# Three more PSUM banks for the MoE groups of a fused attention and two-MoE kernel, from the attention's end on

## The chip, the cores and the metric

The kernel runs on one core of one Trainium2 chip, in one launch. The metric is the device time in microseconds (us). The kernel before takes 1096.97 us, the median of three runs (1094.63 to 1098.74).

## What is computed

An attention with rotary position embedding (4 batches, 8 heads, 576 positions, 64 dimensions per head), and behind it two MoE blocks on its 2304 tokens of 512 numbers each. All in float32:

```python
def _attn_ref(q, k, v):
    ...
    q_rot, k_rot = (rotate(q), rotate(k))
    scores = scale * np.matmul(q_rot, k_rot.transpose(0, 1, 3, 2))
    scores = scores - np.max(scores, axis=-1, keepdims=True)
    attn = np.exp(scores)
    attn = attn / (np.sum(attn, axis=-1, keepdims=True) + 1e-09)
    return np.matmul(attn, v).astype(np.float32)

def _moe_ref(x, w1, w2, w3, w_out):        # d_ff = 768
    h = np.maximum(np.maximum(x @ w1, x @ w2), x @ w3)
    return (h @ w_out).astype(np.float32)

def _moe2_ref(x, w_in, w_out):             # d_ff = 2048
    h = x @ w_in
    g = h * (1.0 / (1.0 + np.exp(-h)))
    return (g @ w_out).astype(np.float32)
```

## The kernel before

**Numbers in two halves.** Every float32 operand of a MoE is kept as a high and a low float16 half of the scaled number, and a product is three float16 matmuls (high by high, high by low, low by high) that add up in PSUM. GpSimd or ScalarE makes the high half (`split`, L154 and L156), VectorE the low one (L159).

**Groups.** `group` (L502 to L506) takes a tile of one PSUM bank (128 x 512 float32) and adds a list of matmuls up in it. All matmuls of both MoEs but those of the last product are made by it, so they all have line 505. Its bank comes from the ring `ps_m`, which has two. The same ring serves `all_max` (L112), which finds the largest number over all partitions for a scale.

**PSUM has eight banks.** During the attention two are `ps_m`'s, three hold the scores (`ps_s`, one tile), two the transposes (`ps_t`), one the product with v (`ps_x`). The last three pools are closed with the attention (L879). `ps_o` (L899, three banks, for the last product) takes three of those six afterwards.

**The attention** goes tile by tile through scores (L354 to L364), maximum (L374, VectorE), exponential (L381, ScalarE), norm (L393), transposes (L422) with their copies (L426, L428), and the product with v (`av`, L437 to L447).

**The first MoE** (`moe1`) works on one batch at a time, in two halves of 256 and 320 tokens. `up(half, f)` makes three groups of 12 matmuls for each of six pieces f of d_ff, one for each of w1, w2, w3. The first result is read out of PSUM by ScalarE (`t`, L521), the other two by VectorE (`t`, L523), which takes the maximum with the t before. Then the halves of h are made: the high one by ScalarE (L529), the low one by VectorE (L530). `down(half)` makes four groups of 18 matmuls from h, read by ScalarE (`y`, L547) and stored in DRAM. Batch 3 runs in this order: up(0, f) for six f, up(1, 0), down(0), up(1, f) for the other five f, down(1). While it runs, the weights of the second MoE are loaded (L688) and split (L690), one piece for each group (L889 to L897), and its first block of 512 tokens is loaded (L703) and split (`y_split`).

**The second MoE** (`moe2`) takes five blocks of tokens (four of 512, one of 256). `s1` makes 16 groups for a block; ScalarE reads each with the Silu (`gt`, L735), VectorE makes both halves of g from it (L158, L159). `s2` makes the last product for 128 tokens at a time, 48 matmuls of 512 columns in a bank of `ps_o` (L749); VectorE reads it (`ob`, L751), and a DMA stores it (L762).

**What sets the order.** The source gives the data flow and a program order. The tile framework lays the instructions into each engine's queue when the kernel is built: of what is ready by its own model of time, the earlier in the program goes first. So the queue of an engine can differ from the program order, and it can change when buffers are added. A pool's memory is given to a later pool once the tiles in it have had their last reader.

Of the kernel before, what the change touches and what calls it, by code (L numbers as in the profile page):

```python
# [7 lines left out]
F32 = mybir.dt.float32  # L8
# [6 lines left out]
PSUM = bass.MemoryType.PSUM  # L15
DRAM = bass.MemoryType.DRAM

P = 128
# [4 lines left out]
def fused_kernel(  # L23
# [51 lines left out]
    ps_m = Ring(ctx, "ps_m", 2, space=PSUM)  # L75
# [423 lines left out]
    w1_scale = {}  # L499
    WO1 = Weights(wp1, "wo1", NF1, DM)  # L500

    def group(passes, n):  # L502
        ps = ps_m.tile([P, 512], F32, tag="m", name="m")
        for i, (l, r) in enumerate(passes):
            nc.tensor.matmul(ps[:, 0:n], l, r, start=(i == 0), stop=(i == len(passes) - 1))  # L505
        return ps  # L506

    def moe1(b, pools):
# [5 lines left out]
        def up(half, f):  # L514
            o, n = PARTS[half][:2]
            part = []

            def evac(e, ps):
                t = tmp_p.tile([P, n], F32, tag="t", name="t")
                if e == 0:  # L520
                    nc.scalar.activation(out=t, in_=ps[:, 0:n], func=AF.Copy, scale=2.0 ** -22)  # L521
                else:
                    nc.vector.scalar_tensor_tensor(  # L523
                        out=t, in0=ps[:, 0:n], scalar=2.0 ** -22, in1=part[-1], op0=ALU.mult, op1=ALU.max
                    )
                part.append(t)
                if e == 2:
                    hh = h1[half, f] = h1_p.tile([P, 2, n], F16, tag="h1", name="h1")
                    nc.scalar.activation(out=hh[:, 0], in_=t, func=AF.Copy)  # L529
                    nc.vector.tensor_tensor(out=hh[:, 1], in0=t, in1=hh[:, 0], op=ALU.subtract)  # L530

            for e in range(3):
                passes = []
                for c in range(KC):
                    i, fo = (f // FG * KC2 + c // 2) * 3 + e, (c % 2 * FG + f % FG) * P
                    wh, wl = W1.h(i)[:, fo:fo + P], W1.l(i)[:, fo:fo + P]
                    passes += [(wh, x[:, c, 0, o:o + n]), (wh, x[:, c, 1, o:o + n]), (wl, x[:, c, 0, o:o + n])]
                yield half, n * len(passes), False
                ps = group(passes, n)
                evac(e, ps)  # L540

        def down(half):
            o, n = PARTS[half][:2]

            def evac(m, ps):
                ysb = pools[2].tile([P, n], F32, tag="y", name="y")
                nc.scalar.activation(out=ysb, in_=ps[:, 0:n], func=AF.Copy, scale=cy_t[b])  # L547
                nc.sync.dma_start(out=yscr[:, m, b * S + o:b * S + o + n], in_=ysb)

            for m in range(KC):  # L550
                passes = []
                for f in range(NF1):
                    wh = WO1.h(f)[:, m * P:(m + 1) * P]
                    wl = WO1.l(f)[:, m * P:(m + 1) * P]
                    h = h1[half, f]
                    passes += [(wh, h[:, 0]), (wh, h[:, 1]), (wl, h[:, 0])]
                yield half, n * len(passes), True
                ps = group(passes, n)
                evac(m, ps)
# [160 lines left out]
    def moe2(st, pools, ps_o, wi_rest, wo_all):  # L720
# [3 lines left out]
        def s1(j, f):  # L724
            yt, sg, ch = yts[j]
            n = blocks[j][1]
            wi = st["wi"]
            passes = []
            for c in range(KC):
                i, fo = (f // 4) * KC + c, (f % 4) * P  # L730
                wh, wl = wi.h(i)[:, fo:fo + P], wi.l(i)[:, fo:fo + P]
                passes += [(wh, yt[:, 0, c]), (wh, yt[:, 1, c]), (wl, yt[:, 0, c])]
            ps = group(passes, n)
            gt = gt_p.tile([P, n], F32, tag="gt", name="gt")
            nc.scalar.activation(out=gt, in_=ps[:, 0:n], func=AF.Silu, scale=ch)  # L735
            g = gs[j, f] = g_p.tile([P, 2, n], F16, tag="g", name="g")
            split(g[:, 0], g[:, 1], gt, sg, "dve")
# [139 lines left out]
    for _ in wprep3:  # L877
        pass
    attn_pools.close()  # L879
    while nxt[0] < B - 1:  # L880
        nxt = next(moe)
    w2_p = Ring(ctx, "w2_p", 1, side="right")
# [62 lines left out]
```

## Time and profile before

| | |
|---|---|
| median of three runs | 1096.97 us (1094.63 to 1098.74) |
| the profiled execution | 1101.35 us, its span 1099.6 us |
| mean granted TensorE clock | 0.963 |
| TensorE busy | 1011.0 us (92% of the span) |
| VectorE, ScalarE, GpSimd busy | 570.9, 486.9, 241.9 us |
| last matmul of the attention | near 643 us |
| first matmul of the second MoE | 718.35 us |

The engines are called PE (TensorE matmul), PEld (TensorE's load of weights), DVE (VectorE), ACT (ScalarE), POOL (GpSimd) and SP (the queue that issues DMAs) in the rows. The granted clock is a share of 2.4 GHz, so 0.50 is 1.2 GHz. Matmuls are pipelined, so that a row's duration is a little longer than its distance to the next. The time of a run holds 1 to 2 us around the span.

### The profile page before, as it was taken

To read this page: it belongs to the slowest core of one execution; us is meant where nothing else is said; L and a number is where in the kernel's file an instruction comes from. 1 tells how busy PE (TensorE), PEld (TensorE's weight loads), DVE (VectorE), ACT (ScalarE), POOL (GpSimd) and SP (SyncE) were. 2 spreads that over 40 slices of the span, in tenths; PEclk is the share of its full clock that TensorE was granted. 3 is DMA by queue.
4 is the path that set the end of the run, shared out by engine and by line. 5 is a ranking of instruction groups with operands and counts; after the bars stand their busy time and mean duration, and the time that the engine had idled before them with its cause. 6 is when DMAs were issued, how large, how long until landed. Compare 5 with 4: busy or idle time off the path is not lost.

```text
span 1099.6 us, 16116 instructions
## 1 busy us (share of the span) xinstructions
PE 1011.0 (92%) x6138; PEld 628.7 (57%) x6138; DVE 570.9 (52%) x1124; ACT 486.9 (44%) x1184; POOL 241.9 (22%) x259
## 2 busy tenths in 40 slices
PE   2478898999988999989999888999999999999997
PEld 1244675676775766757767566644444444444554
DVE  5868666434587465466456568424434223423322
ACT  3678675655756567646666731122112012101111
POOL 1595126620146631041111116100000000000000
PEclk9589997999999899989999999999999999999999
DMA  7633032300334423122223263000101000100000
GB/s 193 194 108 125 13 92 50 103 1 7 103 90 133 116 88 100 43 85 87 64 87 105 78 274 129 7 19 5 54 10 49 20 20 1 39 20 1 20 20 20
DMA packets 79389, 76.09 MB, mean 69 GB/s; under 512 B 44752, under 2 KB 61648, under 8 KB 78288
## 3 DMA queue, kind: packets, MB, share of 16 engines
q1 hardware_dynamic: 75760, 65.03, 19.6%
q10 hardware_dynamic: 3552, 10.03, 2.7%
q8 instruction: 48, 0.79, 0.3%
q14 instruction: 29, 0.24, 0.1%
HBM read 57.21 MB, written 17.83 MB: 68 GB/s over the span
## 4 chain that ended last, share of the span: by engine, by line
PE 73%; DVE 4%; POOL 3%; DMA 2%; issue 1%; SPq 1%; ACT 0%; DVEq 0%; POOLq 0%
PE m L505 36%; PE o L749 17%; PE xp L441 6%; PE s L364 5%; PE tr L422 4%; POOL wi L156 1%; PE xp L437 1%; DVE wi L159 1%; PE s L361 1%; PE tr L328 1%; PE s L354 1%; POOL qk L316 1%; DVE nb L374 1%; POOL w L312 0%; SPq L272 0%
## 5 line engine op out<-in xcount | busy, mean ns | idle before, releaser
L505 PE MATMUL m<-x,w 128*128 128x320 f16 (+1 forms) x1632 | 232.6, 290 | 9.9 <-DVE t L523 6.6
L749 PE MATMUL o<-wo,g 128*128 128x512 f16 x828 | 193.2, 379 | 0.0
L505 PEld LDWEIGHTS <-w 128*128 128x128 f16 x1632 | 160.0, 99 | 55.6 <-issue 15.7
L505 PE MATMUL m<-yt,wi 128*128 128x512 f16 (+1 forms) x920 | 189.8, 358 | 0.0
L735 ACT ACTIVATE gt<-m,ch 128x512 f32<-128x512 f32 (+1 forms) x80 | 51.5, 644 | 297.0 <-PE m L505 282.6
L749 PEld LDWEIGHTS <-g 128*128 128x128 f16 x864 | 84.5, 98 | 99.7
L505 PEld LDWEIGHTS <-wi 128*128 128x128 f16 x920 | 89.7, 98 | 89.3
L374 DVE TENSOR_REDUCE nb<-s 128x2 f32<-128x1152 f32 (+1 forms) x80 | 98.8, 1235 | 64.7 <-PE s L364 48.2
L381 ACT ACTIVATE e<-s,nb 128x576 f32<-128x576 f32 x144 | 105.3, 737 | 44.4 <-DVE nb L374 40.0
L158 DVE TENSOR_SCALAR g<-gt,sg 128x512 f16<-128x512 f32 (+1 forms) x80 | 36.7, 458 | 162.9 <-ACT gt L735 162.9
L422 PE MATMUL tr<-ident,e 128*128 128x128 f32 x576 | 100.5, 292 | 17.3 <-ACT pt L426 4.6
L393 ACT ACTIVATE e<-e,rec 128x576 f32<-128x576 f32 x144 | 104.3, 767 | 19.1 <-DVE rec L391 18.9
L207 POOL TENSOR_SCALAR z<-z 128x256 uint16<-128x256 uint16 x64 | 54.9, 857 | 258.6 <-DVE z L206 240.2
L422 PEld LDWEIGHTS tr<-ident,e 128*128 128x128 f32 x576 | 70.5, 148 | 39.6 <-ACT pt L426 9.7
L364 PE MATMUL s<-T 64*128 64x512 f32 (+2 forms) x384 | 85.7, 525 | 0.0
L426 ACT ACTIVATE pt<-tr 128x384 f32<-128x384 f32 x128 | 61.1, 487 | 54.4 <-PE tr L422 53.9
L441 PE MATMUL xp<-pt,vd 128*64 128x256 f32 (+1 forms) x512 | 85.2, 432 | 0.0
L505 PE MATMUL m<-h,wo 128*128 128x256 f16 (+1 forms) x512 | 73.2, 289 | 1.0 <-DVE wo L159 1.0
L364 PEld LDWEIGHTS s<-T 64*128 64x128 f32 x384 | 47.4, 200 | 28.6 <-issue 7.9
L523 DVE SCALAR_TENSOR_TENSOR t<-m,t 128x256 f32<-128x256 f32 (+1 forms) x96 | 43.3, 451 | 38.4 <-PE m L505 35.6
L505 PEld LDWEIGHTS <-wo 128*128 128x128 f16 x512 | 50.0, 99 | 15.8 <-issue 1.8
L441 PEld LDWEIGHTS xp<-pt,vd 128*64 128x64 f32 x512 | 37.2, 141 | 35.5 <-issue 18.8
(174 smaller groups left out, 1146.6 us busy)
## 6 DMA issues: line engine op xcount, KB each, us to landing
z<-in_moe_w_in_dram SPq DMA_DIRECT2D x32, 256.0 KB, 3.1
z<-in_moe_w_out_dram SPq DMA_DIRECT2D x32, 256.0 KB, 3.1
w<-in_moe_w_dram ACTq DMA_DIRECT2D x6, 768.0 KB, 7.4
wo<-in_moe_w_dram ACTq DMA_DIRECT2D x6, 768.0 KB, 4.6
qk<-in_q_dram SPq DMA_DIRECT2D x32, 128.0 KB, 3.1
qk<-in_k_dram SPq DMA_DIRECT2D x32, 128.0 KB, 3.0
vd<-in_v_dram SPq DMA_DIRECT2D x16, 256.0 KB, 2.8
zwi<-z SPq DMA_DIRECT2D x32, 128.0 KB, 2.9
```

The costliest lines, as they stand in the source:

```text
L207: nc.gpsimd.tensor_scalar(out=q[:, :, 2], in0=q[:, :, 1], scalar1=step, scalar2=off, op0=ALU.mult, op1=ALU.add)
L364: nc.tensor.matmul(s[0:n, o:o + m], qs[r], kt[r, a:a + m], start=True, stop=True)
L374: x = nc.vector.tensor_reduce(out=nb[:, 0:m], in_=s[:, 0:576 * m].rearrange("p (h k) -> p h k", h=m), op=ALU.max, axis=AX.X, negate=True)
L381: x = nc.scalar.activation(out=e[:, HK[g]], in_=s[:, HK[g]], func=AF.Exp, bias=nb[:, g:g + 1], accum_out=sm[:, g:g + 1])
L393: nc.scalar.activation(out=e[:, HK[g]], in_=e[:, HK[g]], func=AF.Copy, scale=r[:, g:g + 1])
L422: nc.tensor.transpose(tr[:, i * n:(i + 1) * n], e[0:n, c * P:(c + 1) * P], ident[0:n, 0:n])
L426: nc.scalar.activation(out=to, in_=of, func=AF.Copy)
L441: nc.tensor.matmul(xp[r, 0:n], v4[:, g, c, :], pt[:, c + 5 * g, :], start=False, stop=(c == 3))
L505: nc.tensor.matmul(ps[:, 0:n], l, r, start=(i == 0), stop=(i == len(passes) - 1))
L523: nc.vector.scalar_tensor_tensor(out=t, in0=ps[:, 0:n], scalar=2.0 ** -22, in1=part[-1], op0=ALU.mult, op1=ALU.max)
L735: nc.scalar.activation(out=gt, in_=ps[:, 0:n], func=AF.Silu, scale=ch)
L749: nc.tensor.matmul(ps, l, r, start=(f == 0 and i == 0), stop=(f == NF2 - 1 and i == 2))
```

## The change

A second ring, `ps_g`, of three PSUM banks is made right after the attention's pools are closed. From then on `group` takes a bank of it for three of five groups in turn, and of `ps_m` for two. `all_max` stays with `ps_m`. `ps_o`, made later, gets the three banks that are then left.

```diff
+    ps_g, wide_n = [], [0]
+
     def group(passes, n):
-        ps = ps_m.tile([P, 512], F32, tag="m", name="m")
+
+        wide_n[0] += 1
+        ring, tag = (ps_g[0], "mg") if ps_g and wide_n[0] % 5 > 1 else (ps_m, "m")
+        ps = ring.tile([P, 512], F32, tag=tag, name=tag)
         for i, (l, r) in enumerate(passes):
...
     attn_pools.close()
+    ps_g.append(Ring(ctx, "ps_g", 3, space=PSUM))
     while nxt[0] < B - 1:
         nxt = next(moe)
```

## Rows read from the trace of the kernel before

**Rows 1.** Stretches: busy us of PE, PEld, DVE, ACT, POOL, granted clock, DMA share, GB/s

```profile
620.00:630.00 10.00, 6.83 (x39) 3.72 (x38) 5.48 (x15) 7.49 (x22) 0.77 (x1) 1.00 0.10 32
630.00:635.00 5.00, 4.91 (x21) 3.63 (x20) 2.52 (x11) 3.77 (x8) 0.00 (x0) 0.50 0.01 3
...
643.00:690.00 47.00, 38.05 (x315) 30.61 (x314) 39.95 (x65) 9.37 (x21) 25.10 (x29) 1.00 0.54 213
690.00:718.30 28.30, 27.95 (x207) 20.03 (x205) 9.05 (x18) 5.35 (x12) 2.67 (x4) 1.00 0.05 19
718.30:1093.00 374.70, 374.70 (x1836) 179.32 (x1835) 124.85 (x237) 62.31 (x98) 0.00 (x0) 1.00 0.07 19
```

**Rows 2.** Timeline of TensorE: start, duration, line, operation, count [idle before <-releaser]

```profile
646.04 1.47 PE L505 MATMUL m<-x,w 128*128 128x256 f16 x12 [0.40 <-DVE t L523]
...
650.08 2.78 PE L505 MATMUL m<-x,w 128*128 128x256 f16 x24 [0.21 <-DVE t L523]
654.49 1.47 PE L505 MATMUL m<-x,w 128*128 128x256 f16 x12 [1.63 <-ACT t L521]
...
673.28 0.38 PE L505 MATMUL m<-h,wo1f 128*128 128x256 f16 x2 [1.01 <-DVE t L523]
...
675.72 0.38 PE L505 MATMUL m<-h,wo1f 128*128 128x256 f16 x2 [0.30 <-DVE t L523]
...
688.50 0.43 PE L505 MATMUL m<-x,w1f 128*128 128x320 f16 x2 [1.84 <-DVE t L523]
...
689.72 18.51 PE L505 MATMUL m<-x,w 128*128 128x320 f16 x135
...
713.46 0.43 PE L505 MATMUL m<-h,wo1f 128*128 128x320 f16 x2 [0.34 <-ACT y L547]
```

**Rows 3.** Groups by line (643 to 720 us), waits (640 to 720): us, times, longest

```profile
L159 DVE SCALAR_TENSOR_TENSOR wi<-wi,swis 128x512 f16<-128x512 f32 x15 | 14.9, 994 | 3.9 <-POOL wi L156 3.8
L159 DVE SCALAR_TENSOR_TENSOR wo<-wo,swos 128x512 f16<-128x512 f32 x15 | 11.5, 765 | 3.1 <-POOL wo L156 3.1
...
POOL wi L156 <- DVE wi L159: 12.3, 14, 2.0
...
PE m L505 <- DVE t L523: 7.3, 9, 1.8
```

**Rows 4.** Timeline of VectorE: two reads of t and one h

```profile
656.71 0.41 DVE L523 SCALAR_TENSOR_TENSOR t<-m,t 128x256 f32<-128x256 f32 x1
...
670.07 0.41 DVE L530 TENSOR_TENSOR h<-t,h 128x256 f16<-128x256 f32 x1
...
687.97 0.48 DVE L523 SCALAR_TENSOR_TENSOR t<-m,t 128x320 f32<-128x320 f32 x1
```

**Rows 5.** Timeline of the attention's tail, all engines

```profile
607.14 0.39 PE L505 MATMUL m<-x,w1f 128*128 128x256 f16 x2
...
631.99 0.74 ACT L381 ACTIVATE e<-s,nb 128x576 f32<-128x576 f32 x1 [0.56 <-DVE nb L374]
...
633.95 2.77 PE L505 MATMUL m<-x,w 128*128 128x256 f16 x12
...
637.53 0.54 SPq L703 DMA_DIRECT2D yr<-yscr  x1
...
640.54 2.38 PE L441 MATMUL xp<-pt,vd 128*64 128x320 f32 x16
...
645.12 0.54 DVE L445 SCALAR_TENSOR_TENSOR x<-xp,vs,x 128x320 f16<-128x320 f32 x1
```

**Rows 6.** The second MoE's Silu (groups of the whole span), two of its groups, the last reads

```profile
L735 ACT ACTIVATE gt<-m,ch 128x512 f32<-128x512 f32 (+1 forms) x80 | 51.5, 644 | 297.0 <-PE m L505 282.6
...
900.48 5.34 PE L505 MATMUL m<-yt,wi 128*128 128x512 f16 x24
...
1093.62 1.41 DVE L751 TENSOR_SCALAR ob<-o,co 128x512 f32<-128x512 f32 x2 [2.24 <-PE o L749]
```

## Prediction

> **What bounds the kernel now.** I read the busy time by stretches first, because the change touches nothing before the attention's end. From 718 us to 1093 us TensorE is busy for the whole 374.7 us at a granted clock of 1.00 [rows 1]: the second MoE runs its matmuls back to back, and a wait that isn't there can't be removed. From 643 to 690 us it is busy for 38.05 of 47 us, from 690 to 718 us for all but 0.35 us [rows 1]. So what more PSUM can give lies between the attention's end and 690 us, in the first MoE's last batch (batch 3).
>
> The timeline of TensorE for that stretch says what those 9 us are [rows 2]. Each bracket is idle time just before a group's first matmul, with its releaser. There are eleven from 646 to 713 us. Nine, 7.3 us in all, end with a VectorE read of a group's result into t (L523) [rows 3], one of 1.63 us with the ScalarE read into t (L521), one of 0.34 us with the ScalarE read into y (L547) [rows 2]: together 9.3 us. That is the sign of a bank that isn't free: matmul inputs come from h (L530) or x, not from t. The reader should see that TensorE always stands one group behind the reader of the bank before the last.
>
> Why the reader is late is in the groups by line and the waits [rows 3]: in the same stretch VectorE also makes the low halves of the second MoE's weights (L159), 15 + 15 of them at 994 and 765 ns, 26.4 us in all, in a ping-pong with GpSimd, which waits 12.3 us for VectorE. VectorE is busy 39.95 of the 47 us [rows 1]. In its in-order queue the reads of t stand behind these.
>
> **The change part by part.** It removes no instruction and adds none. Batches 0 to 2 make 3 x (18 + 4 + 18 + 4) = 132 groups; the counter is then at 133 for batch 3's first group, 133 mod 5 = 3, so the first two groups take new banks, the next two the old, and each group takes the bank of the group five before it.
>
> *The waits, with the order of all engines kept.* A group can start when the group five before it has been read, not two before. A group of 12 x 256 columns costs 2.78 - 1.47 = 1.31 us, one of 12 x 320 columns 18.51 / 135 x 12 = 1.65 us, one of 18 x 256 columns 1.31 x 1.5 = 1.97 us [rows 2]. VectorE's times stay, since from 648 to 690 us it waits for GpSimd and not for TensorE. The first idle begins at 646.04 - 0.40 us; less the 0.16 us by which a row overlaps the next (1.47 - 1.31), the next group could start at 645.5 us. Eight groups of 1.31 bring it to 656.0; the ninth (f = 5, e = 0) needs the bank that VectorE frees at 656.71 + 0.41 = 657.12 us [rows 4], a wait of 1.2. Three groups of 1.31 and three of 1.65 bring it to 666.0 us. Now comes down(0), whose input is the last h: VectorE writes it at 670.07 + 0.41 = 670.5 us [rows 4]. No bank helps there. So down(0) starts at 670.5 and not at 673.28 [rows 2]: 2.8 us gained of the 6.8 idle before it (9.3 less 0.30, 1.84 and 0.34). Four groups of 1.97 and six of 1.65 bring TensorE to 688.3, where the seventh needs the bank read at 687.97 + 0.48 = 688.45 [rows 4], a wait of 0.2. The idles of 0.30, 1.84 and 0.34 go. Sum: 2.8 + 0.30 + 1.84 + 0.34 - 0.2 = 5.1 us. This is what three more banks give if VectorE does all as before.
>
> *The waits, with the order made anew.* The order of each engine's queue is made when the kernel is built, from what is ready when. TensorE has f = 5's last group 3 to 4 us earlier, so its t and h are ready earlier than the splits that now stand before them, and the splits have time: the first of them is used at 718 us. If every read followed its group, all 9.3 us would go. I take the middle, 5.1 + 4.2 / 2 = 7.2 us, since the only large rest (4.5 us at down(0)) hangs on seven or eight places in one queue.
>
> *The hand-over of the banks.* The new banks lie where the scores' tile was, if the pools stack. Its last reader is the exponential at 631.99 + 0.74 us, and the first group behind that starts at 633.95 us in the kernel before [rows 5]; so the banks are there in time. Batch 3's first two groups run inside the attention's tail, the first at 607.14 us [rows 5], and now have to wait for 632.7 us. The third and fourth, in the old banks, are as ready as they were and can go in their place: cost 0. If they don't, 2 x 1.31 = 2.6 us of matmuls move behind 632.7 us, where TensorE has no room. A gain has no row that would allow it. I take 0 and keep 2.6 for the range.
>
> *ps_o moves* to the banks of the transposes and of xp, last read at 645.12 + 0.54 us [rows 5], 80 us ahead of its first use. Nothing waits. The small maxima (all_max) stay in the two old banks; block 0's held one of two for 2.6 us and now holds one of five: part of the idles counted above.
>
> *The second MoE.* A group of 512 columns takes 5.34 / 2 = 2.7 us there, its ScalarE read 0.64 us [rows 6]; two banks were enough, five change only which matmuls go first. At the end the two last output tiles end together, 1093.62 us, 1.41 us for both [rows 6]. If the groups run further ahead, the first tile's read is over sooner and only the second's (1.41 / 2 = 0.7 us) and half of the stores stand behind the last matmul: 0 to 1.0 us with the stores, an estimate, taken as 0.
>
> So the sum is 7.2 us, from 2.5 (5.1 - 2.6) to 10.3 (9.3 + 1.0). The profiled execution took 1101.35 us with a span of 1099.6 and would come to 1094.2; it stands 4.4 us over the median of 1096.97. The difference is the same for the median: 1096.97 - 7.2 = 1089.8 us.
>
> **A rule against it.** The granted clock stayed at 1.00 from 643 to 690 us through ten of these gaps, and fell to 0.50 only from 630 to 635 us, after ten microseconds in which TensorE was busy 6.83 [rows 1]. The Trainium skill (TensorE: Matmul & The Clock Gate, "A second HAM failure mode: psum-queue depth-cycling") tells of a kernel in which cycling through banks made micro-idles between groups often enough that the clock went down and up again. By the row the sum stays as it is; by the page moe1's stretch could run partly at 1.2 GHz.
>
> **The rivals.** *Splits first.* VectorE, not PSUM, is the limit from 648 to 690 us. If the new order puts more splits ahead of the t reads, as TensorE's being ahead leaves no one waiting in the builder's eyes, down(0) starts at 673.3 us as before and only 0.30 + 1.84 + 0.34 = 2.5 us come back: 1094.5 us, with 1092 to 1098 around it. For it speaks VectorE's 39.95 of 47 us; against it that t's reads go before splits in the program. A lost place in the attention's tail (2.6 us) ends here too. This is also the case in which the change doesn't do what it says: TensorE's waits on t turn into waits on h.
>
> *Late banks.* The slower one. If the new banks come only when the whole attention is done (last read 645.66 us) and not with the scores (632.73), then the five groups that the kernel before runs from 633.95 to 645.5 us cannot run there, but for what fits into two old banks. 5 x 1.31 = 6.6 us move behind 645.7; and TensorE, idle in 634 to 640 us, stays at the low clock, where a group takes 2.77 and not 1.47 us [rows 5]: 1.3 us for each of two groups. 9.2 us lost against 2.5 regained later: 1103.7 us. It decides at the start of the first matmul into a new bank: 633 or 646 us. Against it: the load of yr, into SBUF that is given out after the attention's end, is issued at 637.53 us, 3 us ahead of the last xp matmuls [rows 5], so memory passes on tile by tile. For it: no row shows a PSUM bank passed on.
>
> *The clock.* Gaps between groups bring the clock down in moe1's last 28 us (690 to 718 us), which at 1.2 GHz would take up to twice as long: 1097 + 28 = 1125 us at most. Against it: there are gaps now and none costs clock, and the change takes gaps away. The Trainium skill's page above is what speaks for it.
>
> **How the numbers follow.** The forecast (1086.7 to 1092) has 0.54; splits first 0.30; late banks 0.14; the clock 0.02. About 0.5% (5.5 us) is what a measurement of this kernel can tell from no change, so faster means under 1091.5 us and slower over 1102.5. Of the forecast 0.50 lies under 1091.5; of splits first 0.02: faster 0.52. Slower has late banks with 0.12 and the clock with 0.02: 0.14. The rest is 0.34. The range from 1086 to 1099 takes in the forecast and splits first, and with that 0.84; the chance of a wrong size at its edges takes it to 0.8.
>
> **What the profile will show.** Right: TensorE busy over 44 of the 47 us after 643 us; no idle released by DVE t L523 over 0.5 us; one idle ahead of the first m<-h,wo group, released by DVE h L530, of 0 to 4.5 us; the second MoE's first group at 710 to 714 us instead of 718.35. Splits first: that idle is over 5 us. Late banks: no m matmul between 634 and 640 us and a clock of 0.5 beyond 640. Wrong in another way: idle time on TensorE after 718 us, where I count none, or the attention's tail ending later than 643 us.

## The result and the profile after

The kernel after takes 1085.55 us (median of six runs, 1082.73 to 1089.01) against 1097.86 us for the kernel before beside it (1094.63 to 1100.92): a ratio of 0.9887, interval 0.9867 to 0.9907. It is faster by 12.3 us where 7.2 us had been forecast. A second measurement of the same two programs, among the experiments below, gave 1090.14 against 1096.46 us, a ratio of 0.9936 (0.9913 to 0.9959), 6.3 us. The two intervals don't overlap, and what sets the two measurements apart is open. Taken together they leave a size between 4 and 15 us, with medians of 6.3 and 12.3, and no closer from the times alone.

To see where it comes from, both profiles are cut at the same four events. The first is an anchor: the start of the third-last group of scores (line 361, s<-kd) before the attention's last product with v. The instructions of TensorE, VectorE, ScalarE and GpSimd in the traces are the same in both kernels up to there, and in the same order; the first that differs is a group of batch 3 on TensorE, at 607.14 us before and 599.67 us after. The others are that last product (xp<-pt,vd), the first group of the second MoE, and the end of the last matmul.

Stretches of the kernel after, as in [rows 1]: busy us of PE, PEld, DVE, ACT, POOL, granted clock, DMA share, GB/s:

```profile
598.18:633.68 35.50, 32.29 (x225) 22.71 (x225) 20.03 (x54) 24.68 (x68) 3.73 (x5) 1.00 0.22 66
633.68:700.81 67.13, 62.96 (x494) 47.62 (x493) 47.90 (x79) 13.82 (x31) 27.45 (x32) 1.00 0.43 170
700.81:1076.27 375.46, 375.46 (x1838) 179.46 (x1835) 126.97 (x238) 61.96 (x98) 0.00 (x0) 1.00 0.07 20
1076.27:1081.00 4.73, 0.00 (x0) 0.00 (x0) 0.75 (x1) 0.00 (x0) 0.00 (x0) 0.90 0.24 55
```

The same four stretches of the kernel before:

```profile
605.65:639.91 34.26, 30.30 (x180) 20.28 (x181) 18.10 (x50) 23.70 (x66) 3.79 (x5) 0.90 0.23 68
639.91:718.35 78.44, 69.15 (x540) 52.05 (x538) 49.52 (x83) 14.75 (x33) 27.77 (x32) 1.00 0.37 146
718.35:1093.80 375.45, 375.45 (x1838) 179.49 (x1835) 125.03 (x238) 62.31 (x98) 0.00 (x0) 1.00 0.06 19
1093.80:1099.60 5.80, 0.00 (x1) 0.00 (x0) 1.23 (x2) 0.00 (x0) 0.00 (x0) 0.82 0.39 90
```

Three things are to be seen. From the anchor to the end it is 493.95 us before and 482.82 us after, 11.1 us less. The anchor itself lies at 605.65 us before and at 598.18 us after: 7.5 us of difference between the two spans arose where no instruction of these engines differs. And of the 11.1 us nothing lies in the second MoE's matmuls (375.45 and 375.46 us), 1.07 us behind the last matmul, and the rest in the first two stretches.

In the first stretch TensorE does 45 more matmuls in 1.24 us more. Its timeline in the kernel after (start, duration, line, operation, count) shows what they are:

```profile
621.57 0.38 PE L116 MATMUL m<-amax,ones 1*128 1x1 f32 x2 [1.11 <-DVE amax L115]
621.88 0.39 PE L510 MATMUL mg<-x,w1f 128*128 128x256 f16 x2
...
622.43 2.24 PE L510 MATMUL mg<-x,w 128*128 128x256 f16 x19
...
628.55 1.47 PE L510 MATMUL mg<-x,w 128*128 128x256 f16 x12
...
633.68 0.70 PE L437 MATMUL xp<-pt,vd 128*128 128x320 f32 x2
...
654.16 0.38 PE L510 MATMUL mg<-h,wo1f 128*128 128x256 f16 x2
...
675.79 1.79 PE L510 MATMUL mg<-x,w 128*128 128x320 f16 x12 [3.83 <-DVE t L528]
...
681.18 5.05 PE L510 MATMUL mg<-x,w 128*128 128x320 f16 x36 [0.34 <-DVE t L528]
```

The new banks (mg) are used from 621.88 us on, 0.3 us after the end of the last exponential (620.83 + 0.74):

```profile
620.83 0.74 ACT L381 ACTIVATE e<-s,nb 128x576 f32<-128x576 f32 x1 [0.62 <-DVE nb L374]
```

In the attention's last 12 us TensorE now runs groups of batch 3 between the transposes: 8.75 groups are done when the last product with v begins, 5 in the kernel before. 3.75 groups of 1.31 us are 4.9 us of work, done in 1.24 us more than in this profile of before (in 2.8 us more between the second profiles, 35.64 and 32.84 us). The clock stays at 1.00, where it was down to 0.50 in [rows 1] and a group took 2.77 us in [rows 5]; over the stretch that cost at most 34.26 x (1 - 0.90) = 3.4 us (in the second profile of before, 5 x 0.05 + 5 x 0.29 from 622 to 632 us, at most 1.7 us).

In the second stretch the idles of 9.3 us [rows 2] have become two of 4.17 us. Before the larger one VectorE's timeline reads:

```profile
660.62 0.48 DVE L535 TENSOR_TENSOR h<-t,h 128x320 f16<-128x320 f32 x1
661.61 1.17 DVE L159 SCALAR_TENSOR_TENSOR wi<-wi,swis 128x512 f16<-128x512 f32 x1 [0.51 <-POOL wi L156]
...
672.41 2.27 DVE L146 TENSOR_REDUCE ym<-yr 128x1 f32<-128x2048 f32 x1
674.60 0.73 DVE L159 SCALAR_TENSOR_TENSOR wo<-wo,swos 128x512 f16<-128x512 f32 x1
675.26 0.48 DVE L528 SCALAR_TENSOR_TENSOR t<-mg,t 128x320 f32<-128x320 f32 x1
```

From 661.61 to 675.26 us VectorE has ten splits of the second MoE's weights and a maximum of 2.27 us in its queue, and no read of t. Five banks fill up behind that as two did [rows 3], only later; the idle of 3.83 us ends with this read.

Behind the last matmul, two reads of output tiles that stood together at 1093.62 us [rows 6] are apart:

```profile
1065.95 0.75 DVE L756 TENSOR_SCALAR ob<-o,co 128x512 f32<-128x512 f32 x1 [8.93 <-PE o L754]
1076.31 0.75 DVE L756 TENSOR_SCALAR ob<-o,co 128x512 f32<-128x512 f32 x1 [9.61 <-PE o L754]
```

### The profile page after: what moved, and what is told of

Its sections match the earlier page's. It is cut to its first block, busy times and chain, and to the rows that moved or that the text cites. A ratio compares the mean times of both kernels' runs of the same rounds, so it can differ in the third digit from the quotient of the medians.

```text
span 1081.0 us, 16103 instructions
## 1 busy us (share of the span) xinstructions
PE 998.1 (92%) x6138; PEld 621.1 (57%) x6138; DVE 570.2 (53%) x1124; ACT 486.0 (45%) x1184; POOL 241.7 (22%) x259
## 4 chain that ended last, share of the span: by engine, by line
PE 72%; DVE 4%; POOL 2%; DMA 2%; issue 2%; SPq 1%; ACT 0%; DVEq 0%; POOLq 0%
PE m L510 24%; PE o L754 17%; PE mg L510 12%; PE xp L441 5%; PE s L364 4%; PE tr L422 4%; PE xp L437 1%; POOL wi L156 1%; PE s L361 1%; PE tr L328 1%; PE s L354 1%; DVE wi L159 1%; SPq L272 1%; DMA z<-in_moe_w_in_dram 1%; DMA z<-in_moe_w_out_dram 1%
## 5 line engine op out<-in xcount | busy, mean ns | idle before, releaser
L510 PE MATMUL m<-x,w 128*128 128x256 f16 (+1 forms) x1380 | 197.0, 287 | 6.7 <-DVE t L528 4.1
L754 PE MATMUL o<-wo,g 128*128 128x512 f16 x828 | 184.6, 379 | 0.0
L740 ACT ACTIVATE gt<-mg,ch 128x512 f32<-128x512 f32 (+1 forms) x48 | 31.0, 646 | 240.4 <-PE mg L510 232.0
L510 PE MATMUL mg<-yt,wi 128*128 128x512 f16 (+1 forms) x552 | 113.6, 359 | 0.0
L422 PE MATMUL tr<-ident,e 128*128 128x128 f32 x576 | 98.2, 287 | 11.8 <-ACT pt L426 2.7
L756 DVE TENSOR_SCALAR ob<-o,co 128x512 f32<-128x512 f32 x18 | 13.5, 751 | 161.8 <-PE o L754 161.8
L364 PE MATMUL s<-T 64*128 64x512 f32 (+2 forms) x384 | 83.1, 510 | 0.0
L510 PE MATMUL m<-yt,wi 128*128 128x512 f16 (+1 forms) x368 | 74.8, 355 | 0.0
L510 PE MATMUL m<-h,wo 128*128 128x256 f16 (+1 forms) x448 | 64.2, 286 | 2.1 <-POOL wo L156 1.0
```

The costliest lines, as they stand in the source:

```text
L364: nc.tensor.matmul(s[0:n, o:o + m], qs[r], kt[r, a:a + m], start=True, stop=True)
L422: nc.tensor.transpose(tr[:, i * n:(i + 1) * n], e[0:n, c * P:(c + 1) * P], ident[0:n, 0:n])
L754: nc.tensor.matmul(ps, l, r, start=(f == 0 and i == 0), stop=(f == NF2 - 1 and i == 2))
```

## Experiments

The theory after this result had three parts: the banks give TensorE work in the attention's tail, which is a lead of some 5 us and keeps the clock up; they bridge VectorE's splits in batch 3; and in the second MoE they are worth the 1 us at the end. The rivals were that one of these does it alone, and that VectorE's queue, not PSUM, is the cause. All diffs are against the kernel after unless they say otherwise.

The table has for each kernel the ratio of its times with its interval, the difference of the medians, and four readings of its profile: the time from the anchor to the end, its difference to 493.3 us (the mean of the two profiles of before, 493.95 and 492.66), and TensorE's idle time from the anchor to the second MoE's first group, that of the attention's tail plus that of batch 3.

| kernel | ratio | medians, us | anchor to end, us | less 493.3 | idle, us |
|---|---|---|---|---|---|
| before (first profile) | | | 493.95 | +0.6 | 4.0 + 9.3 |
| before again | 1.0000 (0.9979 to 1.0022) | +0.3 | 492.66 | -0.6 | 4.1 + 9.4 |
| after | 0.9887 (0.9867 to 0.9907) | -12.3 | 482.82 | -10.5 | 3.2 + 4.2 |
| after again | 0.9936 (0.9913 to 0.9959) | -6.3 | 484.10 | -9.2 | 3.4 + 3.9 |
| new banks in the second MoE only | 0.9989 (0.9967 to 1.0012) | -0.7 | 490.56 | -2.7 | not comparable |
| new banks in batch 3 only | 0.9927 (0.9898 to 0.9956) | -6.7 | 484.99 | -8.3 | 3.3 + 3.8 |
| new banks from batch 3's 13th group on | 0.9923 (0.9897 to 0.9949) | -8.2 | 485.00 | -8.3 | 4.0 + 4.7 |
| new banks for batch 3's first ten groups only | 1.0011 (0.9989 to 1.0033) | +0.8 | 494.02 | +0.7 | 3.2 + 10.6 |
| one new bank, not three | 0.9925 (0.9897 to 0.9953) | -6.9 | 486.09 | -7.2 | 3.1 + 6.7 |
| before, eight matmuls more in the tail | 0.9997 (0.9976 to 1.0018) | +0.2 | 491.14 | -2.2 | 2.7 + 9.2 |
| before, splits of w_out late | 0.9968 (0.9937 to 1.0000) | -3.4 | 488.38 | -4.9 | 4.0 + 4.3 |
| before, both of these | 0.9950 (0.9931 to 0.9969) | -4.8 | 485.87 | -7.4 | 2.7 + 4.4 |
| after, splits of w_out late | 0.9883 (0.9855 to 0.9912) | -12.4 | 478.21 | -15.1 | 3.0 + 0 |
| the same again | 0.9866 (0.9833 to 0.9899) | -14.7 | 478.42 | -14.9 | 3.4 + 0 |

**Where the banks work.** First, the banks in one place alone:

```diff
-    ps_g, wide_n = [], [0]
+    ps_g, wide_n, on = [], [0], [False]
...
-        ring, tag = (ps_g[0], "mg") if ps_g and wide_n[0] % 5 > 1 else (ps_m, "m")
+        ring, tag = (ps_g[0], "mg") if on[0] and wide_n[0] % 5 > 1 else (ps_m, "m")
```

with `on[0] = True` ahead of the call of `moe2`:

> The three new banks serve the second MoE only; batch 3 of the first MoE keeps the two old ones. If the gain has three places (the attention's tail, the waits of batch 3, the very end), this keeps only the end: the profile of after has 4.7 us from its last matmul to the end of the span where before has 5.8, so 1.1 us faster than before, about 0.1%, with the waits of 9.3 us on TensorE still there. If the second MoE's own order matters more (it was remade altogether), several us faster. If only the waits of batch 3 matter, 0.

or with `on[0] = True` behind the making of `ps_g` and `on[0] = False` ahead of `moe2`:

> The three new banks serve batch 3 only; the second MoE goes back to two. Three places: all of the gain of about 12.3 us but the 1.1 us at the end, so 11.2 us faster, 1.0%. The tail of the attention is as in after, the granted clock stays at 1.00 there. If the second MoE's order matters, clearly less than 11.

Batch 3 alone has -6.7 us, the second MoE alone -0.7 us with an interval around none. The end behind the last matmul is 4.7 us in every kernel with new banks in the second MoE but 5.8 us in this one of batch 3 alone, in the one with the first ten groups alone, and in all with the banks of before: that 1.07 us belongs to the banks in the second MoE. In the second MoE's own kernel the queue's order changed as well: its first groups were put into batch 3, at 650.69 us, where a bank and an input were free:

```profile
650.69 0.81 PE L510 MATMUL mg<-yt,wi2f 128*128 128x512 f16 x3
```

So it isn't a pure test of the second MoE, and the stretches can't be compared for it; its time can.

**Lead or bridge.** To tell the lead of the attention's tail from the bridging of waits later, the banks were given to a part of batch 3's groups only. In the loop that makes one group after the other (`n` counts them), `on[0] = n > 11`:

> The new banks serve from the twelfth group of batch 3 on; the first eleven, which hold all that runs inside the attention's tail, keep two banks. The waits of before ahead of the twelfth group (0.40, 0.47, 0.21, 1.63 us) stay, 6.6 us of waits can go, of which after kept 4.2, and the end gains 1.1. If the tail is a place of the gain of its own (3.7 us of 11.1 in the two profiles): 3 to 6 us faster than before, and the granted clock falls to 0.50 near 630 us as in before. If the waits after the attention are all that matters, as the prediction had it: 7 us faster or more, whatever the tail does.

or from the making of `ps_g` on, and `on[0] = n < 10` in the loop, so that they stay off later:

> The new banks serve the first nine groups of batch 3 only, those that after runs inside the attention's tail; all later ones have two, the second MoE too. The counterpart of the run with the banks from the twelfth group on. If the tail is a place of its own: the granted clock stays at 1.00 there (3.4 us in the execution that was profiled before, less where the clock falls for less long), the waits behind the attention stay at 6 to 9 us, the end stays at 5.8 us: 2 to 5 us faster than before. If only the later waits matter: 0 to 1 us.

`n` is counted up behind each group, so the setting holds from the group after it. The first run has the new banks from the 13th group on (its first group in one is the 15th) and the second for the first ten, six of which take a new bank. Both are one off the count that the expectations give (the twelfth, and nine).

The first of the two isn't the test that it was meant to be. Its later groups, with their banks free, were laid ahead into the attention's tail, and the clock stayed at 1.00 there as in the kernel after:

```profile
626.77 2.35 PE L510 MATMUL mg<-x,w 128*128 128x256 f16 x20
```

The other is a clean one. Its tail has TensorE's instructions of the kernel after in the same order and takes as long (35.44 us to the last product with v, 35.50 there), so it has all of the lead:

```profile
608.38:643.82 35.44, 32.29 (x225) 22.64 (x226) 20.03 (x54) 24.60 (x68) 3.70 (x5) 1.00 0.23 67
```

But the time is that of the kernel before. The lead is given back in batch 3, where TensorE stands in waits for t again (engine, what it waited for: us in total, times, longest):

```profile
PE m L510 <- DVE t L528: 8.9, 6, 4.4
```

and the clock falls at the longest of them. TensorE's timeline, and three stretches:

```profile
688.62 0.69 PE L510 MATMUL m<-x,w1f 128*128 128x320 f16 x2 [4.36 <-DVE t L528]
```

```profile
683.00:688.00 5.00, 1.26 (x10) 0.78 (x8) 4.41 (x5) 0.00 (x0) 2.20 (x4) 0.93 0.00 0
688.00:693.00 5.00, 4.38 (x17) 2.52 (x17) 3.95 (x7) 0.91 (x2) 2.83 (x4) 0.50 0.01 2
693.00:698.00 5.00, 5.00 (x35) 3.39 (x33) 3.47 (x6) 0.47 (x1) 1.85 (x4) 0.89 0.02 3
```

A lead alone is therefore worth nothing here, or at most 1096 x 0.0011 = 1.2 us by the interval. It stays in the kernel after, where the banks bridge what TensorE meets later, VectorE's queue.

**How many banks.** One new bank, so that three are taken in turn:

```diff
-        ring, tag = (ps_g[0], "mg") if ps_g and wide_n[0] % 5 > 1 else (ps_m, "m")
+        ring, tag = (ps_g[0], "mg") if ps_g and wide_n[0] % 3 > 1 else (ps_m, "m")
...
-    ps_g.append(Ring(ctx, "ps_g", 3, space=PSUM))
+    ps_g.append(Ring(ctx, "ps_g", 1, space=PSUM))
```

> One new bank instead of three, one group of three in it. If what counts in the attention's tail is that some group is there to run, the clock stays at 1.00 from the fourth to the eighth us behind the last scores, and the 1.1 us at the end come too; the waits behind the attention, which need three groups of lead, come back at some 7 us: 5 to 6 us faster than before. If one bank is all that is needed: as after, 11 us. If the tail needs the three: 1 to 3 us faster.

The first new bank brings 7.2 us, where three bring 9.2 to 10.5 us (profiles); the times (-6.9 us, and -6.3 and -12.3) don't tell them apart. Idle time in batch 3 is 6.7 us, between before and after, in many short waits instead of a long one; in the tail its clock is 1.00.

**The clock in the tail.** Eight matmuls, added to the kernel before behind the last scores:

```diff
+        if (b, hp, o) == (B - 1, NP - 2, 256):
+            warm()
+
+    def warm():
+        xp = ps_x.tile([P, 512], F32, tag="xp", name="xp")
+        for i in range(8):
+            with tc.issue_after(last["xp"]):
+                nc.tensor.matmul(xp, W1.h(0)[:, 0:P], W1.h(0)[:, 0:512], start=True, stop=True)
```

> The kernel before with eight matmuls of 512 columns more (1.7 us, their result is never read) in TensorE's idle time inside the attention's tail, near 626 us. If the clock is what the tail lost: the granted clock stays at 1.00 from 630 to 637 us, where before had 0.50 for 6.8 us, and 3.4 us come back less up to 1 us of delay: 2 to 3.4 us faster than before. If the low clock was a chance of one execution, or hidden: 0 to 1.7 us slower.

They filled the gap (1.89 us from 624.41 us on), the clock was 1.00 in the whole tail, and its profile is 2.2 us shorter than those of before from the anchor to the end:

```profile
603.16:636.35 33.19, 30.46 (x200) 20.22 (x200) 18.55 (x51) 23.79 (x66) 3.80 (x5) 1.00 0.23 71
```

It isn't a test of the clock alone, since the order of the tail was made anew with it: six groups of batch 3 are done there, not five. The times show no difference (+0.2 us, interval of about 2.3 us to either side). What the low clock of the tail costs in the time is thus not settled: by the lower end of the interval the filler brings at most 1096 x 0.0024 = 2.6 us.

**VectorE's queue.** The second MoE's output weights are split one piece for each of batch 3's later groups, among the reads of t. Here VectorE splits all 16 only behind the last h of batch 3; no bank is added or taken:

```diff
-                    nc.vector.tensor_tensor(out=hh[:, 1], in0=t, in1=hh[:, 0], op=ALU.subtract)
+                    last["h"] = nc.vector.tensor_tensor(out=hh[:, 1], in0=t, in1=hh[:, 0], op=ALU.subtract).ins
...
-            W.split(i)
+            if nm == "wo":
+                with tc.issue_after(last["h"]):
+                    W.split(i)
+            else:
+                W.split(i)
...
-        if n > WI.m:
-            next(wo_prep, None)
```

On the kernel after, and on the kernel before:

> The changed kernel, with the 16 splits of the last product's weights (wo) queued on VectorE behind the last h of batch 3 instead of among its reads of t. If VectorE's queue is what holds up the rest: the idle of 3.8 us that after has before up(1, 2), and the 0.3 behind it, go, and 4 us are gained over after (about 1081.5 us where after took 1085.6), 1.4% under before. If something else holds it (the ring of four t tiles, h, GpSimd's half of the wi splits), the idle stays and the time is that of after.

> The kernel before with the same move of the wo splits, and its two banks. If the reader is late because of the splits, then most of the 9.3 us of waits go without any bank: 4 to 6 us faster than before (the first 3 us of them fall before the wo splits begin and stay). If two banks are too few whatever VectorE does: waits of 7 us or more stay, 0 to 2 us faster.

With two banks, as before, and TensorE's order that of the kernel before up to the second MoE, the idle time in batch 3 falls from 9.3 to 4.3 us, as far as three more banks bring it. So one and the same wait can be halved from either side. The whole stretch, from 637.67 to 710.50 us, and its two largest waits for t:

```profile
637.67:710.50 72.83, 68.50 (x539) 52.07 (x538) 39.84 (x73) 15.11 (x33) 16.86 (x22) 1.00 0.40 157
```

```profile
PE m L505 <- DVE t L523: 2.5, 5, 1.2
...
PE m L505 <- ACT t L521: 1.5, 1, 1.5
```

The time follows less clearly: -3.4 us, with no gain at the edge of the interval. GpSimd's halves of the same splits move along (16.86 us of its work are in this stretch, 27.77 before), and VectorE's splits of w_in wait for GpSimd too [rows 3]. So the two runs show what the splits of w_out cost in the queues of both engines, and not VectorE's part alone.

With late splits and three more banks, nothing is left. From the last product with v on TensorE is busy without a gap:

```profile
635.22:697.79 62.57, 62.57 (x494) 47.66 (x493) 37.57 (x69) 13.81 (x31) 17.02 (x22) 1.00 0.46 182
697.79:1073.25 375.46, 375.46 (x1838) 179.52 (x1835) 134.92 (x249) 61.96 (x98) 8.63 (x10) 1.00 0.07 20
```

(This is the second profile of that kernel.) Ten of the 16 splits lie in the second MoE now, where VectorE has 134.92 and not 126.97 us of work in 375.46 us, and cost TensorE nothing there.

**Again, on one chip.** The kernel after, this version, the kernel before, and the kernel before with late splits and the eight matmuls:

> The changed kernel as it is, for a second profile and to stand beside the next one on one chip. 10 to 13 us faster than before (0.9887 in the first measurement); the idle of some 3.8 us before up(1, 2) and a clock of 1.00 in the attention's tail, as in its first profile, if these belong to the order and not to one execution.

> The changed kernel with the splits of wo queued behind the last h, again, beside the changed kernel on the same chip. From the scores at the common place to the end it was 4.6 us shorter than after in one profile (478.2 against 482.8 us), so 3 to 5 us faster than after if that shows in the medians; if the start's scatter or a cost in the second MoE takes it, 0 to 1 us.

> The kernel before itself, for a second profile. If the fall of the clock in the attention's tail belongs to the order of the work: it falls to 0.50 again near the last scores, for 3 to 7 us. If it was a chance: 1.00 throughout. Time as before.

> The kernel before with both: the eight matmuls more in the attention's tail (1.7 us, their result is never read) and the splits of wo behind the last h; two banks. If the tail's clock is worth its 3.4 us once VectorE's queue no longer takes it back: 2 to 3 us faster than with the late splits alone, so 7 to 9 us faster than before. If the tail is worth nothing: as with the late splits alone, 3 to 5 us.

The kernel after with late splits is the fastest: 1081.72 against 1090.14 us for the kernel after on the same chip, and the intervals of the ratios don't overlap (0.9833 to 0.9899, 0.9913 to 0.9959). The first measurement of the kernel after (0.9867 to 0.9907) does overlap with it. From the anchor to the end it is 4.4 to 5.9 us shorter, whichever of the two profiles of each are compared. Late splits with the filler and two banks have -4.8 us, late splits alone -3.4 us; these intervals overlap, so that the filler's part is open here too.

The second profile of the kernel after has the anchor at 606.30 us, 8.1 us later than the first, with the same program. The second profile of before has it at 602.44 us, 3.2 us earlier than its first. Over all fourteen profiles it lies between 598.18 and 608.38 us. Most of the 8.1 us is the clock: from 100 us to the anchor TensorE is busy 7.3 us longer with the same instructions, at a mean granted clock of 0.97 and not 0.99. The first profile of after, and the second:

```profile
100.00:598.18 498.18, 473.87 (x3338) 336.42 (x3335) 305.40 (x656) 327.53 (x865) 153.68 (x159) 0.99 0.27 79
```

```profile
100.00:606.30 506.30, 481.19 (x3343) 340.33 (x3343) 307.60 (x658) 329.05 (x869) 153.95 (x160) 0.97 0.27 79
```

## Why the prediction was right or wrong

The forecast was 7.2 us faster, 1089.8 us, with a range from 1086 to 1099. The direction was right; the first measurement lies just below the range, the second (1090.14 us) at the forecast. That the second meets it is in part luck, since its terms are not those of the forecast. From the anchor to the end, where chance has less room, the gain is 11.1 us in the first pair of profiles and 492.66 - 484.10 = 8.6 us in the second. So the sum was too small by 1 to 4 us; what of the 12.3 us lies beyond is of the size of the scatter ahead of the anchor.

Of the 11.1 us, 9.3 - 4.2 = 5.1 are waits in batch 3, 0.7 idle time in the tail, at most 3.4 the low clock, 1.07 the end; about 0.8 us has no row. Of the 8.6 us in the second pair, 9.4 - 3.9 = 5.5 are waits, 0.7 idle time in the tail, 1.1 the end, none the clock (1.7 us lost in either, in the tail before and in batch 3 after); 1.3 us has no row. Set against the forecast's terms, the first pair is 7.2 - 2.1 (waits) + 4.1 (tail) + 1.1 (end) + 0.8 = 11.1 us, the second 7.2 - 1.7 + 0.7 + 1.1 + 1.3 = 8.6 us.

- **What bounds the kernel: right.** The second MoE has the same matmul time to 0.01 us.
- **The waits: a term mis-sized, for a reason that was half right.** 7.2 us were taken, 5.1 and 5.5 measured, which is the lower end (5.1) and not the middle. The choice of the middle failed: the new order didn't put the reads of t ahead of the splits. That 5.1 us was also the sum for the old order is luck: that sum left its rest at down(0) and had no lead from the tail in it. "VectorE, not PSUM, is the limit" stood there as the rival's reason, and the experiments bear it out as much as the forecast's: late splits alone remove 5.0 us, banks alone 5.1, both all.
- **Where the rest of the wait lies: wrong.** An idle released by h was expected ahead of down(0). There is none (654.16 us has no bracket). Counted from the anchor, down(0) begins (673.28 - 605.65) - (654.16 - 598.18) = 11.7 us sooner than in [rows 2]: h was made sooner, and TensorE met the ten splits and the maximum later, ahead of a group of up(1, f), in an idle of 3.83 us released by a read of t where none over 0.5 us was to be. TensorE is busy 42.83 us in the 47 us behind the attention, and not over 44:

```profile
636.75:683.75 47.00, 42.83 (x349) 34.02 (x348) 40.26 (x65) 10.27 (x23) 24.19 (x28) 1.00 0.54 213
```

- **The hand-over of the banks: the step that failed.** "A gain has no row that would allow it" was wrong: two rows that stood beside it allow it, 6.83 us busy of 10 and a clock of 0.50 behind that [rows 1]. TensorE was short of work in the tail, groups of batch 3 were ready but for a bank, and banks came free there. It was only asked whether the first groups lose their place. In place of a cost of 0 to 2.6 us it was 3.75 groups of lead for 1.24 us (2.8 us in the second pair), and the clock stayed up: 0.7 us less idle time and at most 3.4 us less of low clock, in a term taken as 0. What this is worth by itself is open, since the lead alone left the time as it was (1.0011) and so did the filler (0.9997).
- **The end: mis-sized.** 0 to 1.0 us by the mechanism that occurred, taken as 0; 1.07 us measured.
- **Splits first** didn't occur as put (2.5 us back, idle over 5 us at down(0)), but its cause is what keeps 3.8 us standing. **Late banks** is refuted: the first matmul into a new bank starts at 621.88 us, 12 us ahead of the last product with v, not behind it. In all eight profiles with new banks in batch 3 that matmul starts 0.14 to 0.31 us behind the end of the last exponential, while transposes still follow. This fits banks that pass on from the scores; the traces don't name the banks.
- **The clock** as a rival would have lost up to 28 us and is refuted: the clock is 1.00 from the anchor to the last matmul in the first profile of after, and the second lost at most 1.7 us. The micro-idles between groups of which the Trainium skill tells (TensorE: Matmul & The Clock Gate, "A second HAM failure mode: psum-queue depth-cycling") aren't borne out here: five banks in turn leave two gaps where two banks had eleven, and where the clock fell in batch 3, a single long idle stood ahead (4.36 us, and 3.88, 3.75 and 2.94 us below), not a string of short ones.

A sentence of the Trainium skill's reads on this case from the other side: consistent bubbles on the engine that should be saturated can mean that there isn't enough SBUF or PSUM for the next tile (Perfetto Trace Analysis, "Optimization Strategy"). The trace agrees that they can, 9.3 to 4.2 us with three more banks, and shows that they need not: 9.3 to 4.3 us with not one more.

## What to carry to other kernels

Where a bank's reader is late, look at what stands ahead of it in its engine's queue before adding banks; here moving work that nobody yet waited for took as much off the waits as three banks (9.3 to 4.3 and to 4.2 us), though less off the time (3.4 us, and 6.3 to 12.3), and both together left no gap in batch 3. When buffers come free in a stretch where the bound engine lacks work, ask what is laid ahead into that stretch, and whether the lead lasts: a lead that runs into the same queue later is given back. Measure a change from the last event that both kernels share, and repeat the kernel itself, before explaining a difference by its edit.

## What was not expected of the hardware

- One program's first 600 us differ by up to 8.1 us from one execution to the next (598.18 and 606.30 us to the anchor), with a mean granted clock of 0.99 and 0.97 on the way.
- With nearly the same idle in the same place the clock can stay or fall. Behind 3.83 us it stayed at 1.00 in the first profile of after; behind 3.88 us in the second it fell, at a cost of 5 x 0.09 + 5 x 0.25 = 1.7 us at most. The two lengths mark no border: it fell behind 3.75 us in the same place with the new banks in batch 3 only (0.66 from 681 to 686 us), and behind 2.94 us with those in the second MoE only (0.66 from 669 to 674 us). The second profile of after:

```profile
684.11 2.43 PE L510 MATMUL mg<-x,w 128*128 128x320 f16 x12 [3.88 <-DVE t L528]
```

```profile
681.00:686.00 5.00, 1.89 (x11) 1.23 (x11) 5.00 (x6) 0.59 (x2) 1.97 (x3) 0.91 0.02 5
686.00:691.00 5.00, 5.00 (x30) 3.21 (x28) 4.49 (x8) 0.41 (x2) 2.81 (x3) 0.75 0.00 0
```

- In the attention's tail the clock fell in all four profiles whose TensorE has no added work behind the last scores (before twice, late splits on two banks, the second MoE's banks only), and in none of the ten others.
